# x transposed by DMA on its way into SBUF, in place of TensorE transposes: a gated mix of a state-space layer and a linear-attention layer

## The chip, the cores and the metric

The kernel runs on one core of a Trainium2 chip. The metric is device time in microseconds (us) of one execution. The time before is the median of four runs; one further execution was taken by the hardware profiler, and the views of it that are quoted here all come from that execution.

## The reference, cut to what matters

One input x (2048 rows by 512 columns, bf16) goes through two branches, and a gate per row mixes them.

```python
g = sigmoid((x * gate_w).sum(-1, keepdims=True))
# branch a: diagonal complex state space, 512 states, recurrence over the 2048 rows
Bu = einsum("bld,pd->blp", x, B_bar)
for t in range(L): h = Lam_bar * h + Bu[:, t]
a = 2 * einsum("blp,dp->bld", hs, Cmat).real + x * Dskip
# branch b: linear attention, 32 heads of 16; phi = [softmax(p), softmax(-p)]
q, k, v = split(x @ wqkv);  pq = q @ w_phi;  pk = k @ w_phi     # per head
kv = einsum("bhsf,bhsd->bhfd", phi(pk), v);  z = phi(pk).sum(s)
o = (phi(pq) @ kv) / (phi(pq) . z + 1e-6)
b = o.reshape(B, S, D) @ wo
out = g * a + (1 - g) * b
```

Every matmul that reads x contracts over its 512 columns, so TensorE needs x with the columns on the partitions: that is the tile `xT`.

## The kernel before, in words

**Rows and phases.** Row r is split as r = 4·(128·a + c) + f: f (0 to 3) is the phase, a (0 to 3) the block, c the partition. `xT[:, kt, f*512 + a*128 + c]` holds column block kt of that row, so the columns of `xT` are ordered by phase first. The scan runs over 512 steps of four rows each.

**Loading x.** SP loads x in its natural layout into `xn` (two tiles that share the memory of `ET0` and `ET1`), block 0 in two halves and then blocks 1 to 3 (L312, L315, L317). For each block and phase `x_block` runs four TensorE transposes (L431) into one PSUM buffer, and VectorE or ScalarE copies that buffer into `xT` (L373, L375): 16 groups of four transposes, 16 copies. Ahead of them six matmuls on a zeroed tile (`NWARM`, L418) run while no data is there, and one more (`NDUM`, L443) follows the first two groups.

**What follows on TensorE.** `v_unit` (L457): 16 groups of four 128x512 matmuls, x times Wv; groups 0 and 1 are split in two halves, so that the first can start with half of Wv. `par` (L493 to L498): nine small matmuls that spread the parameter vectors. `gate` (L904): 64 matmuls of one column. `g_unit` (L685, L690): x times `BT`, needs both halves of `BT` and all four blocks of one phase. `fold` (L665): folds w_phi into Wk and Wq; needs `WT` and the block-diagonal `BD` that VectorE makes. Then `k_unit` (L797, L828), `q_unit` (L888), `smalls` (L955) and `mix` (L997, L1013, L1017, L1029) with the output transfers.

**SP's queue at the start.** The x pieces and half of Wv, then six DMA transposes of 512x512 bf16 (512 KB each): the two of B into `BT` (L321), Wk and Wq into `WT` (L323, L324), the two of C into `ET` (L602), with Wc (L322) and four pieces of Wo (L326) among them. DMAs take turns on eight semaphores, so the ninth waits until the first has landed.

**The order.** Nothing is scheduled on the chip. The list `ORDER` gives, task by task, the order of issue and the engine of each task that could go to two; a small planner (`_Plan`) walks it and assigns buffers. Each engine runs its own instructions in that order and waits on semaphores. Constants such as `d_x` are due times of the loads that the planner uses; they are not waits.

Of the kernel before, what the change touches and what calls it, by code (L numbers as in the profile page):

```python
# [122 lines left out]
def kernel(  # L123
# [47 lines left out]
NWARM = 6  # L171
NDUM = 1
ORDER = (
    8, 10, 14, 13, 26, 174, 22, 176, 18, 166, 170, 25, 21, 190, 173, 162, 17, 158, 169, 202, 192, 178, 206, 165,
    0, 194, 222, 204, 197, 226, 28, 224, 160, 209, 30, 230, 32, 198, 233, 250, 96, 210, 218, 234, 34, 201, 228,
    36, 40, 38, 214, 252, 180, 42, 242, 134, 212, 236, 44, 238, 46, 216, 4, 186, 136, 2, 48, 90, 59, 240, 254,
    244, 220, 812, 182, 62, 810, 140, 75, 188, 83, 61, 138, 678, 814, 142, 55, 184, 98, 69, 680, 430, 156, 434,
    144, 432, 816, 258, 146, 66, 56, 64, 436, 262, 438, 81, 342, 265, 818, 256, 334, 70, 260, 337, 346, 148, 348,
    338, 554, 150, 341, 444, 446, 344, 152, 52, 440, 154, 6, 450, 443, 356, 358, 360, 350, 382, 352, 354, 87, 388,
    50, 449, 362, 364, 85, 384, 820, 392, 528, 556, 522, 366, 390, 272, 386, 368, 394, 370, 490, 396, 372, 530,  # L180
    456, 398, 524, 458, 374, 532, 274, 400, 452, 496, 526, 376, 534, 78, 536, 460, 404, 822, 470, 538, 276, 406,
    414, 378, 92, 380, 540, 472, 462, 417, 408, 426, 454, 494, 544, 492, 266, 73, 475, 498, 500, 464, 284, 286,
    546, 410, 542, 502, 476, 298, 466, 412, 77, 504, 548, 620, 428, 100, 506, 508, 102, 288, 104, 88, 562, 268,
    468, 624, 614, 652, 512, 514, 622, 278, 618, 300, 106, 270, 516, 518, 616, 478, 290, 110, 626, 108, 280, 520,
    480, 282, 302, 628, 114, 656, 558, 630, 292, 418, 654, 112, 564, 550, 294, 246, 402, 482, 422, 304, 248, 566,
    560, 646, 116, 568, 738, 650, 648, 574, 484, 632, 118, 552, 486, 570, 576, 636, 424, 572, 580, 658, 594, 586,
    740, 296, 122, 742, 582, 660, 420, 638, 744, 584, 578, 306, 120, 746, 710, 94, 126, 686, 488, 596, 588, 598,
    124, 698, 640, 308, 310, 748, 688, 634, 690, 770, 130, 662, 750, 590, 510, 682, 700, 642, 128, 702, 684, 644,
    776, 664, 712, 774, 778, 838, 692, 668, 592, 752, 312, 772, 754, 314, 780, 782, 600, 714, 832, 694, 756, 670,
    704, 844, 672, 834, 760, 696, 602, 330, 842, 846, 784, 318, 706, 840, 132, 604, 666, 762, 850, 332, 836, 716,  # L190
    708, 718, 786, 720, 826, 322, 606, 788, 852, 722, 874, 854, 792, 848, 868, 320, 326, 794, 862, 674, 608, 724,
    764, 324, 796, 828, 872, 830, 328, 676, 766, 726, 768, 798, 800, 864, 878, 856, 876, 610, 866, 860, 728, 804,
    808, 870, 802, 892, 880, 894, 896, 806, 730, 758, 884, 904, 902, 900, 732, 858, 898, 906, 886, 1268, 908, 316,
    1000, 890, 882, 1270, 998, 910, 1036, 914, 996, 916, 1274, 1002, 734, 1272, 888, 918, 912, 1262, 920, 922,
    1028, 1004, 1054, 924, 1006, 930, 1074, 1062, 1030, 1022, 1008, 1010, 1056, 1128, 1130, 1076, 1080, 1024,
    1048, 1132, 1032, 612, 1264, 1050, 1256, 1126, 1058, 1026, 1266, 1078, 1082, 1100, 1102, 1034, 1012, 1052,
    1114, 932, 736, 1040, 1060, 1106, 1014, 1084, 1104, 1088, 1108, 1016, 1110, 1018, 1112, 1134, 1020, 1260,
    1038, 1086, 942, 936, 1116, 1136, 926, 1138, 934, 1066, 1276, 1064, 954, 1278, 1142, 944, 1092, 1118, 1204,
    1206, 1042, 1210, 1230, 1258, 938, 1232, 1068, 1236, 1208, 1212, 1234, 1044, 1214, 1090, 1152, 928, 1144,
    1146, 1158, 966, 1238, 1094, 1178, 1070, 1120, 1216, 940, 1154, 1218, 1122, 1280, 1148, 1096, 1222, 1240,  # L200
    1073, 1184, 1180, 1242, 1156, 946, 1186, 1284, 1166, 1282, 1160, 1244, 968, 1188, 1286, 1192, 948, 1288, 1246,
    1150, 1290, 1162, 1384, 1292, 1098, 1182, 1168, 1248, 1296, 1364, 1164, 1386, 970, 1190, 1358, 1125, 1170,
    1366, 1194, 1298, 1250, 1390, 956, 1300, 1360, 1220, 950, 958, 1392, 1302, 1224, 1368, 1196, 1312, 1046, 1306,
    1388, 1362, 1394, 1314, 1172, 1370, 1308, 952, 1338, 960, 1396, 1226, 1174, 1198, 1252, 1332, 1310, 1376,
    1200, 1372, 962, 1346, 1398, 1316, 1334, 964, 1400, 1318, 1340, 972, 1304, 1402, 1202, 1416, 1374, 1255, 978,
    1418, 1336, 1320, 1342, 1436, 980, 1438, 1344, 1378, 1404, 1324, 974, 1420, 1229, 1410, 976, 1442, 1380, 1348,
    982, 990, 1412, 1322, 1326, 1444, 1440, 1406, 1462, 1350, 1414, 1177, 984, 1383, 992, 1468, 1494, 1422, 986,
    1446, 1450, 1464, 1448, 988, 1470, 1428, 1352, 1328, 1496, 1354, 1488, 1476, 994, 1330, 1472, 1466, 1490,
    1424, 1454, 1474, 1140, 1498, 1409, 1492, 1500, 1480, 1356, 1426, 1478, 1452, 1430, 1433, 1456, 1482, 1435,
    1502, 1485, 1504, 1506, 790, 1294, 1458, 1514, 824, 1508, 1460, 1520, 1487, 1522, 1516, 1510, 1518, 1513, 1524)  # L210
# [18 lines left out]
def _fast_path(ctx, tc, A_x, A_Lambda_re, A_Lambda_im, A_B_re, A_B_im, A_C_re, A_C_im, A_log_dt, A_Dskip,  # L229
# [5 lines left out]
    x4 = A_x[0].rearrange("(a c f) d -> a c f d", f=F, c=P)  # L235
# [64 lines left out]
    xn2 = [wk.tile([P, 2, F, D], BF16, tag=f"ET{k}", name="xn", bufs=1) for k in range(2)]  # L300
    xn = [xn2[a // 2][:, a % 2] for a in range(4)]
# [10 lines left out]
    nc.sync.dma_start(out=xn[0][:, 0:2], in_=x4[0][:, 0:2])  # L312
    for k, q in ((0, nc.scalar), (2, nc.sync)):
        q.dma_start(out=Wv[:, k:k + 2, :], in_=B_wqkv[k * P:(k + 2) * P, 2 * D:3 * D].rearrange("(k p) n -> p k n", p=P))
    nc.sync.dma_start(out=xn[0][:, 2:4], in_=x4[0][:, 2:4])  # L315
    for a in range(1, 4):
        nc.sync.dma_start(out=xn[a], in_=x4[a])  # L317
# [26 lines left out]
    pl = _Plan({"DVE": 2.4e3, "ACT": 5.0e3, "PE": 1.1e3, "SP": 32.0e3})  # L344
# [10 lines left out]
    early = [pl.held("ET", k) for k in range(4)]  # L355
# [4 lines left out]
    def bfv(b):  # L360
        return b.t[:].bitcast(BF16)[:, 0:512]
# [17 lines left out]
    d_x = [pl.at(t) for t in (3.9, 5.6, 7.0, 8.6, 10.2)]  # L379
    d_wv, d_b, d_wk, d_wq, d_wo, d_ct = (pl.at(t) for t in (5.3, 19.5, 25.5, 30.5, 33.0, 0.0))  # L380
    d_wv0 = pl.at(4.4)
    d_vec, d_wc = pl.at(10.5), pl.at(21.0)
# [38 lines left out]
    xt = {}  # L421
    dums = []

    def x_block(a):
        pl.unit("x_block")
        for f in range(F):
            b = pl.buf(*A1)

            def tr(e, b=b, f=f):
                for kt in range(KT):  # L430
                    nc.tensor.transpose(bfv(b)[:, kt * P:(kt + 1) * P], xn[a][:, f, kt * P:(kt + 1) * P], ident[:])  # L431
            t = pl.add({"PE": 460.0} if a == 0 and f < 2 else _pe(4, 128), tr, deps=[d_x[a + (a > 0 or f > 1)]], follow=[t_warm], bufs=[b, early[a // 2]])
            if a == 0 and f < 2:
                dums.append(t)
            xt[a, f] = evac_task(xT[:, :, tcols(f, a)], b, lambda b: bfv(b).rearrange("p (k c) -> p k c", k=KT), [t],
                                 ("ACT", "DVE"), bf=True, rank=9)

        if a == 0:
            bd = pl.buf(*A1)

            def dum(e):
                for _ in range(NDUM):
                    MM(out=bd.t[:], lhsT=warm[:, 0:P], rhs=warm[:], start=True, stop=True)  # L443
            t_dum.append(pl.add({"PE": NDUM * 430.0}, dum, follow=dums, bufs=[bd]))

    vt = {}
    t_dum = []

    def v_unit(ti):
        pl.unit("v_unit")  # L450
        f, a = ti % F, ti // F
        b = pl.buf(*A1)

        def mm(k0, k1):
            def fn(e):
                for kt in range(k0, k1):
                    MM(out=f32v(b), lhsT=xT[:, kt, tcols(f, a)], rhs=Wv[:, kt, :], start=(kt == 0), stop=(kt == KT - 1))  # L457
            return fn
        if ti < 2:
            t = pl.add({"PE": 860.0 if ti == 0 else 434.0}, mm(0, 2), deps=[xt[a, f], d_wv0], follow=t_dum, bufs=[b])  # L460
            t = pl.add({"PE": 434.0}, mm(2, 4), deps=[d_wv], follow=[t], bufs=[b])
        else:
            t = pl.add(_pe(4, 512), mm(0, 4), deps=[xt[a, f], d_wv], bufs=[b])
        vt[ti] = evac_task(vx[:, ti, :, 0:Dh], b, lambda b: f32v(b).rearrange("p (h e) -> p h e", e=Dh), [t], ("ACT",), rank=8.5)

    x_block(0)
# [366 lines left out]
    x_block(1)  # L833
    for ti in range(0, 4):
        v_unit(ti)
    x_block(2)
# [858 lines left out]
```

## Time and profile before

| | |
|---|---|
| median of 4 runs | 154.82 us (154.78 to 154.97) |
| the profiled execution, its own time | 154.34 us |
| its span in the profile | 152.3 us |
| busy: PE (TensorE matmul) | 145.7 us, 96% of the span |
| busy: DVE (VectorE) | 134.3 us, 88% |
| busy: ACT (ScalarE) | 110.2 us, 72% |
| granted TensorE clock, mean | 0.995 |

Times inside the profile are counted from the start of the span. PE is TensorE's matmuls, PEld its weight loads, which overlap them; SPq is the part of SP that issues DMAs. A group line gives the source line, the engine, the operation, what is written and read, the count, the busy time and the mean length of one in ns. In a table of windows each engine has its busy time and, in brackets, its instructions; the last three columns are the granted clock, the share of the 16 DMA engines that was busy, and the GB/s that they moved. Matmuls are pipelined, so the 379 ns of one 128x512 matmul is its latency; in a stream four of them take 0.86 us.

### The profile page before, as it was taken

To read this page: it belongs to the slowest core of one execution; us is meant where nothing else is said; L and a number is where in the kernel's file an instruction comes from. 1 tells how busy PE (TensorE), PEld (TensorE's weight loads), DVE (VectorE), ACT (ScalarE), POOL (GpSimd) and SP (SyncE) were. 2 spreads that over 40 slices of the span, in tenths; PEclk is the share of its full clock that TensorE was granted. 3 is DMA by queue.
4 is the path that set the end of the run, shared out by engine and by line. 5 is a ranking of instruction groups with operands and counts; after the bars stand their busy time and mean duration, and the time that the engine had idled before them with its cause. 6 is when DMAs were issued, how large, how long until landed. Compare 5 with 4: busy or idle time off the path is not lost.

```text
span 152.3 us, 3284 instructions
## 1 busy us (share of the span) xinstructions
PE 145.7 (96%) x1173; PEld 85.5 (56%) x1173; DVE 134.3 (88%) x377; ACT 110.2 (72%) x226; POOL 4.3 (3%) x14
## 2 busy tenths in 40 slices
PE   6799999999999999999999999999999999999990
PEld 1465476745665656655544665656556555555570
DVE  2377998998999999999999899999999999999250
ACT  3049999889897889879889997977774392753030
POOL 8300000000000000000000000000000000000000
PEclk9999999999999999999999999999999999999998
DMA  4999989300013141334603222244132634316531
GB/s 129 380 274 212 160 229 225 62 0 0 0 31 76 34 93 55 103 82 110 79 0 101 93 94 86 80 87 65 34 104 68 73 75 97 100 37 118 128 103 45
DMA packets 31147, 14.95 MB, mean 98 GB/s; under 512 B 23192, under 2 KB 30488, under 8 KB 31128
## 3 DMA queue, kind: packets, MB, share of 16 engines
q1 hardware_dynamic: 29280, 13.20, 38.2%
q10 hardware_dynamic: 1752, 1.51, 3.4%
q8 instruction: 10, 0.16, 0.5%
q14 instruction: 9, 0.07, 0.2%
q0 software_dynamic: 96, 0.00, 0.0%
HBM read 3.17 MB, written 2.10 MB: 35 GB/s over the span
## 4 chain that ended last, share of the span: by engine, by line
PE 84%; DMA 5%; DVE 5%; ACT 1%; issue 0%; SPq 0%; DVEq 0%
PE pp L685 18%; PE pp L1013 17%; PE pp L1029 9%; PE pp L797 9%; PE pp L457 8%; PE pp L888 5%; PE pp L997 4%; PE pp L690 3%; DMA Wv<-in_B_wqkv_dram 3%; DMA xn<-in_A_x_dram 3%; PE pp L828 3%; PE pp L1017 2%; DVE c L733 2%; PE pp L431 1%; PE pp L665 1%; DVE KVbd L870 1%
## 5 line engine op out<-in xcount | busy, mean ns | idle before, releaser
L685 PE MATMUL pp<-xT,BT 128*128 128x512 bf16 x128 | 31.9, 381 | 0.0
L1000 ACT CAST late<-pp 128x512 bf16<-128x512 f32 x32 | 17.8, 598 | 10.8 <-PE pp L997 10.7
L1013 PE MATMUL pp<-CT,Gs 128*128 128x512 bf16 (+1 forms) x104 | 23.5, 362 | 0.0
L685 PEld LDWEIGHTS <-BT 128*128 128x128 bf16 x128 | 17.8, 145 | 8.7
L242 ACT ACTIVATE E<-pp 128x512 bf16<-128x512 f32 x32 | 17.8, 613 | 2.1 <-PE pp L797 1.5
L242 ACT ACTIVATE ET<-pp 128x512 bf16<-128x512 f32 x32 | 17.7, 603 | 1.0 <-PE pp L888 0.9
L1034 ACT ACTIVATE late<-pp,Gg 128x512 bf16<-128x512 f32 (+1 forms) x15 | 9.5, 669 | 9.8 <-PE pp L1029 9.8
L1029 PE MATMUL pp<-Wo,late 128*128 128x512 bf16 (+1 forms) x68 | 15.9, 367 | 0.0
L457 PE MATMUL pp<-Wv,xT 128*128 128x512 bf16 x64 | 15.8, 379 | 0.1
L888 PE MATMUL pp<-xT,Wq 128*128 128x512 bf16 x64 | 15.8, 378 | 0.0
L797 PE MATMUL pp<-Wk,xT 128*128 128x512 bf16 x64 | 15.4, 379 | 0.0
L373 ACT CAST vx<-pp 128x512 bf16<-128x512 f32 x16 | 9.3, 595 | 7.9 <-PE pp L457 7.8
L1013 PEld LDWEIGHTS <-Gs 128*128 128x128 bf16 x104 | 9.4, 98 | 7.3 <-DVE Gs L773 0.5
L373 ACT CAST Gs<-pp 128x512 bf16<-128x512 f32 x21 | 12.2, 603 | 1.7 <-PE pp L690 1.7
L1004 DVE TENSOR_TENSOR late<-late 128x512 bf16<-128x512 bf16 x32 | 12.3, 417 | 0.0
L997 PE MATMUL pp<-KVbd,ET 128*128 128x128 bf16 x128 | 10.7, 219 | 0.0
L997 PEld LDWEIGHTS <-ET 128*128 128x128 bf16 x128 | 8.6, 98 | 3.4 <-issue 0.2
L797 PEld LDWEIGHTS <-xT 128*128 128x128 bf16 x64 | 6.1, 98 | 6.7
L821 DVE TENSOR_TENSOR E<-E,rc 128x2048 bf16<-128x2048 bf16 x8 | 9.7, 1219 | 0.1
L888 PEld LDWEIGHTS <-Wq 128*128 128x128 bf16 x64 | 5.9, 97 | 6.3
L733 DVE TENSOR_TENSOR_SCAN c<-sp,c 128x512 bf16<-128x512 f32 x8 | 9.3, 1208 | 0.0
L457 PEld LDWEIGHTS <-xT 128*128 128x128 bf16 x64 | 5.8, 98 | 5.8 <-DVE xT L375 0.4
(173 smaller groups left out, 253.5 us busy)
## 6 DMA issues: line engine op xcount, KB each, us to landing
Zs<-c SPq DMA_DIRECT2D x32, 64.0 KB, 2.1
xn<-in_A_x_dram SPq DMA_DIRECT2D x3, 512.0 KB, 4.8
out_dram<-late ACTq DMA_DIRECT2D x9, 128.0 KB, 2.0
c<-c SPq DMA_DIRECT2D x16, 64.0 KB, 2.0
CT<-ET SPq DMA_DIRECT2D x8, 128.0 KB, 3.6
out_dram<-late SPq DMA_DIRECT2D x6, 128.0 KB, 2.0
xn<-in_A_x_dram SPq DMA_DIRECT2D x2, 256.0 KB, 4.4
Wo<-in_B_wo_dram SPq DMA_DIRECT2D x4, 128.0 KB, 2.7
```

Source lines behind the costliest of these rows:

```text
L242: return nc.scalar.activation(**kw)
L373: nc.scalar.copy(out=o, in_=view(b))
L457: MM(out=f32v(b), lhsT=xT[:, kt, tcols(f, a)], rhs=Wv[:, kt, :], start=(kt == 0), stop=(kt == KT - 1))
L685: MM(out=f32v(b), lhsT=BT[:, kt].rearrange("p r (q t) -> p (r q) t", t=NT)[:, :, j + 4 * h], rhs=xT[:, kt, f * NCH:(f + 1) * NCH], start=( ...
L733: nc.vector.tensor_tensor_scan(out=bw_.t[:, ri], data0=rb, data1=b1.t[:, ri], initial=0.0, op0=ALU.mult, op1=ALU.add)
L797: MM(out=f32v(b), lhsT=xT[:, kt, tcols(f, a)], rhs=Wk2[:, kt, :], start=(kt == 0), stop=(kt == KT - 1))
L888: MM(out=f32v(b), lhsT=Wq2[:, kt, g * P:(g + 1) * P], rhs=xT[:, kt, f * NCH:(f + 1) * NCH], start=(kt == 0), stop=(kt == KT - 1))
L997: MM(out=f32v(pn[sgn])[:, g * P:(g + 1) * P], lhsT=ets[f].t[:, sgn, g, cs], rhs=KVbd[:, sgn, g, :], start=True, stop=True)
L1000: tn = pl.add(_act(512), lambda e, sgn=sgn: nc.scalar.copy(out=o2.t[:, sgn], in_=f32v(pn[sgn])), deps=[t], bufs=[pn[sgn], o2], rank=rank + 2)
L1004: VT(out=v, in0=v, in1=als[f].t[:, a, sgn * H:(sgn + 1) * H].rearrange("p (g h) -> p g h", g=HG).unsqueeze(2).to_broadcast([P, HG, Dh, 8]) ...
L1013: MM(out=f32v(py)[:, 0:w], lhsT=st, rhs=CT[:, tt // 2 + 4 * (tt % 2), n * w:n * w + w], start=(tt == 0), stop=False)
L1029: MM(out=f32v(py)[:, 0:w], lhsT=oT.t[:, g, :], rhs=Wo[:, g, hs], start=False, stop=(g == HG - 1))
```

## The change

x no longer comes in its natural layout. SP issues five DMA transposes that write `xT` directly: phase 0 in two halves of 256 rows, then phases 1, 2 and 3 with 512 rows each. A source row is 1 KB, and the rows of one phase lie 4 KB apart. `xn`, the 64 TensorE transposes, the 16 copies of their results and the extra matmul `NDUM` go; `NWARM` rises from 6 to 8. Both halves of Wv are issued by ACT's queue; before, one was issued by SP. Only the first group of `v_unit` is split. `ET0` and `ET1` are free from the start. The list `ORDER` and the planner's due times are new throughout, so that tasks of every engine stand in another order.

```diff
-NWARM = 6
-NDUM = 1
+NWARM = 8
 ORDER = (
...
-    x4 = A_x[0].rearrange("(a c f) d -> a c f d", f=F, c=P)
+    xf = A_x[0].rearrange("(r f) d -> f r d", f=F)
...
-    xn2 = [wk.tile([P, 2, F, D], BF16, tag=f"ET{k}", name="xn", bufs=1) for k in range(2)]
-    xn = [xn2[a // 2][:, a % 2] for a in range(4)]
...
-    nc.sync.dma_start(out=xn[0][:, 0:2], in_=x4[0][:, 0:2])
-    for k, q in ((0, nc.scalar), (2, nc.sync)):
-        q.dma_start(out=Wv[:, k:k + 2, :], in_=B_wqkv[k * P:(k + 2) * P, 2 * D:3 * D].rearrange("(k p) n -> p k n", p=P))
-    nc.sync.dma_start(out=xn[0][:, 2:4], in_=x4[0][:, 2:4])
-    for a in range(1, 4):
-        nc.sync.dma_start(out=xn[a], in_=x4[a])
+    for k in (0, 2):
+        nc.scalar.dma_start(out=Wv[:, k:k + 2, :], in_=B_wqkv[k * P:(k + 2) * P, 2 * D:3 * D].rearrange("(k p) n -> p k n", p=P))
+    for f, r0, r1 in ((0, 0, NCH // 2), (0, NCH // 2, NCH), (1, 0, NCH), (2, 0, NCH), (3, 0, NCH)):
+        nc.sync.dma_start_transpose(out=xT[:, :, f * NCH + r0:f * NCH + r1], in_=xf[f][r0:r1])
...
-    early = [pl.held("ET", k) for k in range(4)]
+    early = {k: pl.held("ET", k) for k in (2, 3)}
...
-    xt = {}
-    dums = []
-
-    def x_block(a):
...
+    xt = {(a, f): d_x[f + (f > 0 or a > 1)] for f in range(F) for a in range(4)}
...
-        if ti < 2:
-            t = pl.add({"PE": 860.0 if ti == 0 else 434.0}, mm(0, 2), deps=[xt[a, f], d_wv0], follow=t_dum, bufs=[b])
+        if ti == 0:
+            t = pl.add({"PE": 860.0}, mm(0, 2), deps=[xt[a, f], d_wv0], follow=[t_warm], bufs=[b])
...
-    x_block(1)
     for ti in range(0, 4):
         v_unit(ti)
-    x_block(2)
     for ti in range(4, 8):
         v_unit(ti)
-    x_block(3)
     for ti in range(8, 12):
         v_unit(ti)
```

In the new order TensorE's stream begins: eight warm matmuls; group 0 of `v_unit` (first half), group 12, group 0 (second half), group 8, all of phase 0; group 9; `par`; groups 13 and 5; group 2; group 1; 16 gate matmuls; groups 7, 3, 11 (phase 3) and 10; 32 gate matmuls; three groups of `g_unit` (12 matmuls, the first that read `BT`); the first `fold` group; 16 gate matmuls; a `fold` group; a `g_unit` group; two `fold` groups. Groups 4, 6, 14 and 15 come later. On SP the fifth piece of x waits, by its semaphore, until the third has landed.

## The prediction, made before the changed kernel was run

> **What bounds the kernel now.** I read the engines' busy shares first, then the windows of the first 32 us, then the start of the chain of waits, then SP's queue. First the busy shares and the slices:
>
> ```profile
> PE 145.7 (96%) x1173; PEld 85.5 (56%) x1173; DVE 134.3 (88%) x377; ACT 110.2 (72%) x226; POOL 4.3 (3%) x14
> PE   6799999999999999999999999999999999999990
> DVE  2377998998999999999999899999999999999250
> ```
>
> TensorE has no idle slice between the third and the last. It sets the end, so a matmul taken out of its stream counts in full, provided that its data keep up. DVE is nearly as full from about 15 us on. The windows (us, PE, PEld, DVE, ACT, POOL, clock, DMA share, GB/s):
>
> ```profile
> 4.00:8.00 4.00, 3.13 (x31) 1.79 (x30) 1.29 (x5) 0.00 (x0) 0.95 (x2) 1.00 1.05 375
> 8.00:12.00 4.00, 3.70 (x45) 2.54 (x44) 2.85 (x13) 2.35 (x5) 0.00 (x0) 1.00 1.13 275
> 12.00:16.00 4.00, 4.00 (x29) 2.11 (x27) 3.66 (x20) 3.93 (x9) 0.00 (x0) 1.00 1.27 173
> 16.00:20.00 4.00, 4.00 (x37) 2.13 (x36) 3.96 (x16) 3.82 (x11) 0.00 (x0) 1.00 1.04 209
> ```
>
> TensorE waits only before 12 us. The DMA engines are already full there: at 375 GB/s while x comes in naturally, at about 200 GB/s while they transpose. The chain says when TensorE stops waiting and what it does then:
>
> ```profile
> 5.39 4.13 DMA xn<-in_A_x_dram
> 9.56 0.84 PE pp L431 x12
> 10.41 0.86 PE pp L457 x4
> 11.27 0.22 PE pp L431 x4
> ...
> 11.87 0.55 PE pp L431 x8
> ```
>
> From 9.56 us on the chain is TensorE almost without a break. The group of the transposes, SP's issues, and two times from issue to landing:
>
> ```profile
> L431 PE MATMUL pp<-ident,xn 128*128 128x128 bf16 x64 | 5.3, 222 | 1.1 <-DMA xn<-in_A_x_dram 1.1
> 10.68 1.70 SPq L321 DMA_TRANSPOSE BT<-in_A_B_im_dram  x1
> 16.32 2.39 SPq L324 DMA_TRANSPOSE WT<-in_B_wqkv_dram  x1
> 21.48 2.05 SPq L602 DMA_TRANSPOSE ET<-in_A_C_re_dram  x1
> BT<-in_A_B_im_dram SPq DMA_TRANSPOSE x1, 5.9
> ET<-in_A_C_re_dram SPq DMA_TRANSPOSE x1, 4.7
> ```
>
> Six 512 KB transposes are in the kernel already. They price the new ones: SP spends 2.05 to 2.39 us on issuing one that does not wait.
>
> **TensorE's useful stream.** The last matmul of the last tile ends at 148.10 us (L1029 starts at 147.06 and takes 1.04). From 9.56 that is 138.54 us. Of it 32 transposes are 2.05 us (0.84+0.22+0.55+0.22+0.22 in the chain). Eight Wv matmuls were done before 9.56, worth 8 x 0.216 = 1.73. Useful work is 138.54 - 2.05 + 1.73 = 138.2 us. Before, it has an effective start of 148.1 - 138.2 = 9.9 us; the change is worth what it takes off that.
>
> **The new start.** The warm matmuls begin at 1.27 and come 0.43 us apart, so eight end at about 4.7. The first Wv group needs the first half of Wv (landed by about 4.6 before) and 256 rows of x. Transposed, these land no earlier than the natural 256 KB did (3.9: the first transpose starts then) and hardly later than the second Wv half (5.39 in the chain), with which they share the engines. I take 4.9. Two matmuls later (5.3) the stream needs the second half of phase 0; the first 1 MB, Wv and phase 0, should be in between 5.4 and 6.1, and I take 5.8: a wait of 0.5.
>
> **The queue behind it.** Until the first matmul on BT five more 512 KB pieces have to land: phases 1, 2, 3 and both parts of B. Call the time of one c. Bounds: 2.05, the shortest issue that did not wait, and 2.65. The latter is the whole stretch from 9.56 to 28.1 (where traffic ends in windows of half a us), 18.5 us less 2.6 for issuing Wo, over six pieces. The landings in the trace's semaphore records sit around the lower end: B_re 2.1 us after the last of x, Wq 1.9 after Wk, C_im 2.2 after C_re; B_im took 3.6, during which a 16 KB instruction fetch, one packet in the trace, took 1.2 us. I take c = 2.2, since most rows lie there, and allow one such fetch (1.4) as an even chance. The 4 KB pitch of x's rows is not in the trace; Wk and Wq, whose rows lie 3 KB apart, are the nearest and show no surcharge. The fifth piece waits for the third's landing (about 8 us), two pieces ahead of its turn: no cost. So B_im lands at 5.8 + 5 x 2.2 = 16.8, with a fetch 18.2, at c = 2.65 at 19.1, at c = 2.05 at 16.1.
>
> TensorE's work before BT is 12 Wv groups (48 x 0.216 = 10.37), par (0.16) and 48 gate matmuls (3 x 0.38 = 1.14): 11.7 us. It is ready at 4.9 + 0.5 + 11.7 = 17.1. Hence BT matmuls start at 17.1, or with a fetch at 18.3; the useful work left is 138.2 - 11.7 = 126.5. The end of matmuls is 143.6 or 144.8, that is 4.5 or 3.3 us earlier than 148.1. At c = 2.65 it is 19.2 + 126.5 = 145.7, a gain of 2.4. Wk follows B_im by Wc and one piece, 2.4 in all; the three BT groups (2.6) hide that. BD comes out of DVE in time if DVE's parameter chain starts early too: it was done at 22.3, 10.4 us after par's results; now par is at about 9 us, and the mask and swap steps (0.9 us) stand ahead of it, so about 19, with fold due at 19.7.
>
> **The other engines.** The 11 copies on DVE (421 ns each) and 5 on ACT (584 ns) mostly filled idle time: only two on DVE and three on ACT come after par's results. DVE: par's results move from 11.9 to about 9.4, 2.5 us; two copies (0.8), the setup steps moved ahead of par (1.2) and 0.7 of PSUM copies that the new list gives to ACT go, 1.0 of small scalings comes: it can end 2.5 + 0.8 + 1.2 + 0.7 - 1.0 = 4.2 us earlier. ACT: the first Wv copy moves from 8.85 to about 7; three copies go (1.75), two of the folds come (1.2): about 2.4 us earlier in the stretch up to 40 us, where it was busy for 28.9 of 31.2 us. So ACT and DVE allow 2.4 to 4.2 and nearly bind. I charge 0.4 us for waits in the new order that the trace of before cannot show; the bounds are 0 and 2. Ten output transfers went through ACT's queue and seven through SP's; SP now issues five more, 0.53 us each, among transposes of 1.2 us, where it is not full: nothing. C's load lands near 28 as before and is first used at 44.9: nothing. The tail behind the last matmul keeps its form: nothing.
>
> **One rule against, one beside.** Four TensorE transposes take 0.22 us in the stream, 55 ns each, while c is 2.2 us for 16 blocks of 128x128, 138 ns each, on engines that do nothing else at that time. The Trainium skill, "VectorE: DVE Perf Modes", § Rules for kernel authors, says to use TensorE for a 128x128 transpose where a PSUM destination will do; § The three transpose paths gives 390 ns for it and 1309 ns for the DMA. By those figures, taken one at a time, x's 64 blocks would cost the DMA 84 us (an estimate) and the kernel would be far slower; the rows of B, W and C contradict that.
>
> The Trainium skill, "DMA: Bandwidth & Descriptors", § Latency and other measured facts, gives 261 GB/s for a DMA transpose whose middle dimension is not contiguous: 2.0 us a piece, an estimate, by which TensorE would never wait for BT and the gain would be the full 4.5.
>
> **The sum.** Midway between 4.5 and 3.3 is 3.9, less 0.4: 3.5 us. The profiled execution would go from 154.34 to 150.8. The median of the runs was 0.48 above that execution, so I forecast 154.82 - 3.5 = 151.3.
>
> **Rivals.** (1) *Another engine takes over.* DVE is busy for 3.9 to 4.0 of every 4 us between 44 and 60, ACT for 28.9 of 31.2 before 40; TensorE then meets full PSUM buffers or late exps, and only 0.3 to 2.5 us remain: 152.3 to 154.5. For it: the two sums above. Against: both engines also lose work. (2) *The transposed queue is too slow: slower than before.* If the 4 KB pitch, Wv's share or further fetches bring c over 3.1, BT matmuls start after 5.8 + 5 x 3.1 = 21.3, and 126.5 more passes 148. At B_im's own 3.6 they start at 23.8, the matmuls end at 150.3, and the time is 157.0. For it: that one piece. Against: the other five. (3) *No change*, where c is just 3.1 or DVE does not move. That the change does not do what it says can be left out: the new TensorE stream has 63 fewer matmuls, 64 transposes and one extra less two warm ones.
>
> **How the numbers follow.** Forecast (gain 2.5 to 4.8): 0.52. Rival 1: 0.30. No change: 0.04. Rival 2: 0.14. About 0.2%, or 0.3 us, is what a measurement can tell from no change. The range runs from 150.0 (all gains, no waits) to 154.2, which takes in most of rival 1; the forecast's own range is 150.0 to 152.3. Faster 0.82, same 0.04, slower 0.14.
>
> **What would show it.** Right: no L431, first Wv matmul near 4.9, BT matmuls at 17 to 18.3, TensorE full from there, last matmul near 144.6. Wrong: the phases of x landing over 2.7 us apart, TensorE waiting on xT or BT for more than 2 us, or new waits of TensorE on ACT or DVE after 20 us.

## The result: 0.2% slower, and where TensorE waits now

The changed kernel takes 155.13 us (median of 34 runs, 154.15 to 156.34), the kernel before 154.81 on the same chips; the ratio is 1.0022 [1.0011, 1.0034]. The forecast was 151.3, its range ended at 154.2. The profiled execution took 154.94, its span is 152.9.

Two lines of the page of the changed kernel, busy time and TensorE's slices:

```profile
PE 142.8 (93%) x1110; PEld 82.1 (54%) x1110; DVE 128.9 (84%) x368; ACT 108.5 (71%) x219; POOL 4.5 (3%) x14
PE   6489999999999999999999699989999999999990
```

The 64 transposes are gone and TensorE is busy for 2.9 us less, but its row now has lower slices: 4 and 8 at 4 to 12 us, where they were 7 and 9, and a 6 near 87 us, where it was 9. The windows name the stretches (columns as before: us, PE, PEld, DVE, ACT, POOL, clock, DMA share, GB/s):

```profile
4.00:8.00 4.00, 1.59 (x6) 0.23 (x4) 0.76 (x9) 0.00 (x0) 1.21 (x2) 1.00 1.21 251
8.00:12.00 4.00, 3.61 (x24) 1.67 (x23) 0.00 (x0) 0.89 (x2) 0.00 (x0) 1.00 0.99 224
84.00:92.00 8.00, 6.75 (x62) 3.35 (x59) 7.79 (x18) 6.16 (x13) 0.00 (x0) 1.00 0.30 98
```

The last stretch in the kernel before:

```profile
84.00:92.00 8.00, 8.00 (x124) 5.03 (x121) 7.41 (x19) 7.10 (x15) 0.00 (x0) 1.00 0.29 95
```

In 4 to 8 us TensorE works for 1.59 us where it worked for 3.13, and in 84 to 92 for 6.75 where it worked for 8.00. TensorE's timeline tells what each idle time waited for (start, length, line, what, count, and in brackets the idle time ahead and its releaser):

```profile
1.27 3.59 PE L411 MATMUL pp<-warm 128*128 128x512 bf16 x8 [1.27 <-DVE warm L305]
6.41 0.60 PE L426 MATMUL pp<-Wv,xT 128*128 128x512 bf16 x2 [1.54 <-DMA xT<-in_A_x_dram]
7.88 3.20 PE L426 MATMUL pp<-Wv,xT 128*128 128x512 bf16 x14 [0.86 <-DMA xT<-in_A_x_dram]
11.46 0.17 PE L461 MATMUL pp<-ident,vec_n 20*128 20x20 bf16 x1 [0.39 <-issue]
...
20.03 2.79 PE L653 MATMUL pp<-xT,BT 128*128 128x512 bf16 x12
23.16 0.40 PE L633 MATMUL pp<-BD,WT 128*128 128x128 bf16 x4 [0.34 <-DMA WT<-in_B_wqkv_dram]
...
87.89 0.95 PE L920 MATMUL pp<-SM,ET 128*128 128x16 bf16 x32 [1.25 <-ACT ET L240]
...
103.20 1.04 PE L994 MATMUL pp<-Wo,late 128*128 128x512 bf16 x4 [0.39 <-DMA late<-late]
```

The first matmul on x starts at 6.41 (forecast 4.9), the first on BT at 20.03 (17.1 to 18.3), and four later waits add 0.39 + 0.34 + 1.25 + 0.39. The last Wo matmul ends at 148.73 (144.6). ScalarE's queue shows the 0.39 ahead of par in the making:

```profile
6.39 0.25 ACTq L313 DMA_DIRECT2D vec_n<-in_A_Lambda_im_dram  x1
7.85 0.26 ACTq L313 DMA_DIRECT2D vec_n<-in_A_Dskip_dram  x1
8.15 0.49 ACTq L313 DMA_DIRECT2D vec_n<-in_gate_w_dram  x1
```

In the semaphore records the first and second piece of x land at 6.37 and 7.83, 0.02 us before: two of the five 1 KB parameter loads wait for the large pieces whose semaphores they take next, and the fifth stands behind them on the queue. Its own semaphore was free from 4.30 on; it lands at 11.26, and par starts at 11.46. And VectorE's timeline shows what comes ahead of the smalls group (L920), which needs SM:

```profile
83.55 0.69 DVE L691 TENSOR_TENSOR c<-c,Tcs 128x1024 bf16<-128x1024 bf16 x1 [1.22 <-DMA c<-c]
...
85.67 0.43 DVE L835 TENSOR_TENSOR KVbd<-pp,mask 64x256 bf16<-64x256 f32 x1
...
87.58 0.16 DVE L838 TENSOR_TENSOR SM<-pp,mask 64x16 bf16<-64x16 f32 x1
```

The kv matmuls end at 84.05, but VectorE first waits for a transfer of its scan and runs four steps of it; SM is done at 87.74, and TensorE goes on at 87.89. The releaser that the timeline names, ScalarE's ET, ended 0.13 us after SM; the waits of e4 below name SM, and in e15, where SM is early, the smalls start at 85.66 without a wait, while the same run of exponentials goes on to 87.06.

### The profile page after: what moved, and what is told of

Same layout as the page of the kernel before. It is cut to its first block, busy times and chain, and to the rows that moved or that the text cites. A ratio compares the mean times of both kernels' runs of the same rounds, so it can differ in the third digit from the quotient of the medians.

```text
span 152.9 us, 3142 instructions
## 1 busy us (share of the span) xinstructions
PE 142.8 (93%) x1110; PEld 82.1 (54%) x1110; DVE 128.9 (84%) x368; ACT 108.5 (71%) x219; POOL 4.5 (3%) x14
## 4 chain that ended last, share of the span: by engine, by line
PE 78%; DMA 10%; SPq 7%; ACT 1%; issue 0%; DVE 0%
PE pp L978 16%; PE pp L653 16%; PE pp L994 9%; PE pp L765 9%; PE pp L853 8%; PE pp L962 5%; DMA WT<-in_B_wqkv_dram 4%; DMA xT<-in_A_x_dram 4%; PE pp L658 3%; SPq L311 3%; SPq L315 3%; PE pp L796 3%; DMA late<-late 3%; PE pp L426 2%; PE pp L920 2%; PE pp L982 2%
## 5 line engine op out<-in xcount | busy, mean ns | idle before, releaser
L653 PE MATMUL pp<-xT,BT 128*128 128x512 bf16 x128 | 31.3, 380 | 0.0
L240 ACT ACTIVATE E<-pp 128x512 bf16<-128x512 f32 x32 | 17.0, 614 | 1.4 <-PE pp L796 1.3
L426 PE MATMUL pp<-Wv,xT 128*128 128x512 bf16 x64 | 15.1, 379 | 2.4 <-DMA xT<-in_A_x_dram 2.4
L999 ACT ACTIVATE late<-pp,Gg 128x512 bf16<-128x512 f32 (+1 forms) x15 | 10.1, 679 | 8.4 <-PE pp L994 8.2
L765 PE MATMUL pp<-Wk,xT 128*128 128x512 bf16 x64 | 15.9, 379 | 0.0
L969 DVE TENSOR_TENSOR late<-late 128x512 bf16<-128x512 bf16 x32 | 12.8, 416 | 0.3 <-ACT late L965 0.3
L367 ACT CAST Gs<-pp 128x512 bf16<-128x512 f32 x19 | 10.9, 591 | 1.7 <-PE pp L658 1.0
L962 PE MATMUL pp<-KVbd,ET 128*128 128x128 bf16 x128 | 11.2, 219 | 0.0
```

What stands on the lines that cost most here:

```text
L240: return nc.scalar.activation(**kw)
L367: nc.scalar.copy(out=o, in_=view(b))
L653: MM(out=f32v(b), lhsT=BT[:, kt].rearrange("p r (q t) -> p (r q) t", t=NT)[:, :, j + 4 * h], rhs=xT[:, kt, f * NCH:(f + 1) * NCH], start=( ...
L765: MM(out=f32v(b), lhsT=xT[:, kt, tcols(f, a)], rhs=Wk2[:, kt, :], start=(kt == 0), stop=(kt == KT - 1))
L962: MM(out=f32v(pn[sgn])[:, g * P:(g + 1) * P], lhsT=ets[f].t[:, sgn, g, cs], rhs=KVbd[:, sgn, g, :], start=True, stop=True)
L969: VT(out=v, in0=v, in1=als[f].t[:, a, sgn * H:(sgn + 1) * H].rearrange("p (g h) -> p g h", g=HG).unsqueeze(2).to_broadcast([P, HG, Dh, 8]) ...
```

## The experiments

Theory: the removal is worth what was forecast, and it was spent on a later start and on waits of the new order. Rivals: the removal was never worth it, because VectorE or ScalarE would have set the end; or the transposing queue as such is too slow. "Before" is each time the kernel before on the same chip in the same runs. Where an experiment lists no other base, its edit is to the changed kernel.

### The removal alone

**e3.** The kernel before, without the transposes and their copies; Wv reads the natural x, and xT holds a constant from GpSimd.

```diff
-                    nc.tensor.transpose(bfv(b)[:, kt * P:(kt + 1) * P], xn[a][:, f, kt * P:(kt + 1) * P], ident[:])
+                pass
+    nc.gpsimd.memset(xT[:], 0.01)
```

> The kernel before with its own order and its natural load of x, but without the 64 TensorE transposes and the 16 copies: the early Wv groups read the natural tile as if it were transposed, and all later readers of xT get a constant, so the values are wrong. It prices the removal alone. If TensorE's stream is all that counts, what was spent on transposes after 9.56 us (2.05 us) and part of what stood before it goes: 151 to 152.7. If ScalarE or VectorE bind, less than 1 us: above 153.8.

155.81 (1.0054 [1.0036, 1.0072]). It tells nothing of the removal: the large memset held up VectorE's setup, par waited 3.30 us for `sel`, and the clock fell to half for the matmuls that followed. e7 is the same with xT filled from the other two engines.

**e7.**

```diff
+    nc.vector.memset(xT[:, 0:2], 0.01)
+    for kt in (2, 3):
+        for h in range(4):
+            nc.scalar.activation(out=xT[:, kt, h * 512:h * 512 + 512], in_=warm[:], func=ACT.Exp)
```

> The kernel before with its own order list and natural loads of x, but without the 64 TensorE transposes and the 16 copies: xT is filled with a constant instead (half by VectorE, half by ScalarE, before x lands), so its values are not x's. This is the removal alone, with no transposing DMA for x and no new order. Theory 'the matmuls removed count in full on TensorE's stream, and the loss came with the additions': TensorE saves 64 x 55 ns = 3.5 us less what its data make it wait, and the median is 151.0 to 152.8. Rival 'VectorE or another engine would have taken over anyway, so the removal was never worth 3.5 us': 153.5 to 154.6, with new waits of TensorE after 20 us.

153.09 (152.23 to 154.30), 0.986 [0.9806, 0.9915]. The six runs are two groups: 152.23 to 152.25 at a mean granted clock of 0.996 or more, and 153.94 to 154.30 at 0.986. The profiled execution is of the second group; its wait of TensorE on ScalarE, and two of its windows:

```profile
PE pp L459 <- ACT vx L377: 1.6, 1, 1.6
```

```profile
8.00:12.00 4.00, 2.37 (x16) 1.30 (x15) 2.15 (x18) 3.21 (x10) 0.00 (x0) 0.90 1.07 254
84.00:92.00 8.00, 7.89 (x110) 4.80 (x110) 7.41 (x19) 7.01 (x17) 0.00 (x0) 1.00 0.28 89
```

At full clock the removal is worth 155.06 - 152.24 = 2.8 us (three executions), although the fill put 1.6 us of waiting on ScalarE into the start. After 26 us TensorE waits for nothing in the old order: VectorE and ScalarE let this much through. The first rival falls, up to 2.8 us.

### The start

**e1.** x by plain DMA of the same sizes (xT then holds rows, not columns).

```diff
-        nc.sync.dma_start_transpose(out=xT[...], in_=xf[f][r0:r1])
+        nc.sync.dma_start(out=xT[...], in_=A_x[0][f * NCH + r0:f * NCH + r1, :]...)
```

> The changed kernel with its own order, but x comes by plain DMA: the same five pieces of the same size, not transposed, so the values are wrong. Three theories of where the forecast gain went. Q (queue): x lands late because it is transposed, and every later wait follows from that. Then the first Wv matmul starts near 4.9 us instead of 6.41, the first fold near 20 instead of 23.16, the waits at 86 to 88 and 103 us are gone, the last matmul ends near 144.5 instead of 148.7, and the time is near 150.9. P (parameters): the small parameter loads come late and hold back VectorE and ScalarE; then par still starts after 9.5 us, the late waits of 1.7 us stay, and the time is near 152.5. O (order): the new list has its late waits whatever lands when; they stay or grow, 152.5 to 154.

157.83, 1.0201 [1.0155, 1.0246]. The first two pieces land at 4.90 and 6.58 instead of 6.37 and 7.83, so transposing costs 1.2 to 1.5 us there. But the kernel is slower, since ScalarE's queue waits as before, and longer (two lines of the queue, then TensorE's):

```profile
4.92 0.25 ACTq L314 DMA_DIRECT2D vec_n<-in_A_Lambda_im_dram  x1
6.61 0.25 ACTq L314 DMA_DIRECT2D vec_n<-in_A_Dskip_dram  x1
```

```profile
14.10 0.17 PE L462 MATMUL pp<-ident,vec_n 20*128 20x20 bf16 x1 [2.65 <-issue]
```

par waits 2.65 us for parameter loads that were issued at the landings of x, the last at 8.91. So e1 does not price the transposing in the kernel's time: what it brings forward is lost at par. The late wait is there too (1.3 us), so it does not come from the transposes of x.

**e2.** No parameter loads by DMA: `vec_n` is filled with a constant.

```diff
-    for n, src in enumerate(vsrc):
-        nc.scalar.dma_start(out=vec_n[4 * n:4 * n + 4, :], in_=src.rearrange("(j p) -> j p", p=P))
+    nc.vector.memset(vec_n[:], -0.5)
```

> The changed kernel without the five small loads into vec_n: a memset gives constants instead, so the parameters are wrong. With them go their five semaphore turns, so no piece of x waits for another to land. Q: par starts right behind the Wv groups, near 10.9 us instead of 11.46, the last piece of x lands near 13.5 instead of 14.35, a gain of 0.5 to 0.8 us: 154.3 to 154.6. P: VectorE's and ScalarE's chains start earlier, the late waits of 1.7 us go too: 152.8. O: as Q.

154.83, 0.9992 [0.9969, 1.0015], against 1.0022 for the changed kernel: the turns cost 0.3 us by the medians, hardly more than the intervals. The wait at par is gone, but par comes hardly earlier (11.33) in the profile, since most of the 16 matmuls ahead of it ran at half clock:

```profile
6.18 5.22 PE L425 MATMUL pp<-Wv,xT 128*128 128x512 bf16 x16 [1.31 <-DMA xT<-in_A_x_dram]
```

Until 9.4 us they start 0.42 us apart, then 0.21. The late wait stays at 1.3.

**e4.** Wv is not loaded but filled with a constant.

```diff
-    for k in (0, 2):
-        nc.scalar.dma_start(out=Wv[:, k:k + 2, :], in_=...)
+    nc.vector.memset(Wv[:], 0.01)
```

> The changed kernel with Wv filled by a memset instead of its two loads (wrong values). If sharing the DMA engines with Wv is what delays phase 0 (landings 6.39 and 7.85 us), they land near 4.9 and 6.2, the first Wv matmul starts near 5 and the time falls by 1.5 to 2 us, to 153.3. If a transposed piece is slow to start by itself, the first lands after 5.7 and the time falls by less than 0.8 us.

153.01, 0.9868 [0.9826, 0.9909]. The first two pieces of x land at 4.34 and 5.50, where the prediction had put them (4.9 and 5.8); TensorE's timeline, then its waits:

```profile
4.66 3.37 PE L425 MATMUL pp<-Wv,xT 128*128 128x512 bf16 x12
...
21.18 0.40 PE L632 MATMUL pp<-BD,WT 128*128 128x128 bf16 x4
```

```profile
PE pp L919 <- DVE SM L837: 1.2, 1, 1.2
PE pp L993 <- DMA late<-late: 0.6, 1, 0.6
```

Everything up to fold is 1.7 to 2.0 us earlier, the late waits are as before (1.2 and 0.6), and the time is 2.1 us less. Wv's two loads are the largest single cost. That the landings moved is their traffic and not the semaphore turns, since the first two pieces wait for no turn in either kernel; but without the two loads the parameter loads go out by 3.05 us as well, and the wait at par is gone, so the 2.1 us hold both. x is still transposed here, so the second rival, a queue too slow as such, falls for the start.

**e6.** Wv's second half on SP behind the first piece of x; the five parameter loads on GpSimd.

```diff
+        if r1 < NCH:
+            wvd(nc.sync, 2)
...
-        nc.scalar.dma_start(out=vec_n[4 * n:4 * n + 4, :], ...)
+        nc.gpsimd.dma_start(out=vec_n[4 * n:4 * n + 4, :], ...)
```

> The changed kernel with the loads at the start re-queued: the second half of Wv is issued by SP right behind the first piece of x, and the five parameter loads and three gate vectors go to GpSimd's queue, so that they no longer take a turn on the semaphores that the x pieces also use. Theory 'the start was lost to the plain Wv traffic beside the first transposes and to the semaphore turns': the first piece lands by 5.0 instead of 6.39, the first Wv matmul starts by 5.2, par runs at about 10 instead of 11.46, the matmuls on BT start 1 us earlier, and the median is 153.5 (152.8 to 154.2). Rival 'a transposed piece needs its 2.3 us of start-up and 2 us of work whatever else is queued': the second half of x lands later by what Wv is moved behind, about 8.5, TensorE waits there instead, and the median is 154.8 to 155.8.

157.35, 1.0113 [1.007, 1.0156]: the rival. The first piece lands at 5.27, the second only at 8.62:

```profile
8.66 5.96 PE L429 MATMUL pp<-Wv,xT 128*128 128x512 bf16 x14 [2.74 <-DMA xT<-in_A_x_dram]
```

The first Wv matmul starts at 5.32, but the wait moved to the second half of phase 0 and grew, and 14 matmuls then take 5.96 us instead of 3.20, because the clock was at half from 7.46 to 14.29 us.

**e14.** e4, and the two transposes of B left out (BT holds a constant).

```diff
-        nc.sync.dma_start_transpose(out=BT[:, :, ri, :], in_=B_)
+    nc.vector.memset(BT[:].rearrange("p k r q -> p (k r q)"), 0.01)
```

> e4_no_wv_traffic (Wv filled with a constant instead of loaded), and in addition the two transposes of B are left out and BT is filled with a constant by VectorE. TensorE's work is the same; the transposing queue has two 512 KB pieces less ahead of Wk. Theory 'the transposing queue sets fold's start': Wk lands near 16 to 17, TensorE runs from 4.7 to fold without waiting for data, fold starts at 19.7 to 20.3 (e4: 21.18) and the median is 151.6 to 152.1 with the late wait still in it. Rival 'TensorE or VectorE's BD set fold's start, the queue is only close': fold stays at 20.8 to 21.3, median 152.7 to 153.1.

154.09, 0.9973 [0.994, 1.0005], so 1 us slower than e4. It does not decide its question: the fill kept VectorE from `sel`, for which par waited 0.68 us; par ended at 11.2 and fold came at 21.97, with no wait for data from par on. Whether the queue would bind a TensorE that is ready earlier it cannot say.

### The late stage

**e5.** Two q_unit groups go ahead of smalls, two scan steps behind KVbd/SM.

```diff
 ORDER:
-    ... 786, 658, 698 ... 772, 660, 732 ... 736, 792 ... 826, 834 ... 666, 800, 802, 804, 806
+    ... 786, 698 ... 772, 732 ... 736, 658, 660, 792 ... 826, 800, 806, 834 ... 666, 802, 804
```

> The changed kernel with four entries of the order list moved, and nothing else: two q_unit groups of TensorE go ahead of the smalls group that waited 1.25 us near 87 us, and two steps of VectorE's scan chain, which themselves waited 1.22 us for a transfer, go behind the KVbd/SM step that the smalls group needs. Theory 'the new order has waits of its own' (1.25 + 0.4 us of the lost gain): the wait of the smalls group falls from 1.25 to under 0.3 us, the last Wo matmul ends near 147.5 and the median is 153.8 (153.4 to 154.2). Rival 'VectorE or ScalarE sets the end whatever the order of these four': the same 1.2 us come back as waits on VectorE within the next 20 us, and the median stays at 154.8 to 155.3.

155.81, 1.0036 [1.0011, 1.0062]. The wait near 87 is gone, and 1.04 us came back at 94, on ScalarE's exponentials (0.81 and then 0.23):

```profile
94.09 0.26 PE L920 MATMUL pp<-SM,ET 128*128 128x16 bf16 x4 [0.81 <-ACT ET L240]
```

**e13 and e15.** Two kernels with 14 warm matmuls (e8 below); e15 moves the two scan steps as e5 does, and leaves TensorE's order alone.

> e8_warm14 once more, as the base of e15 and e16 on the same chip. If its gain is the clock's, 153.8 (0.99 of before) again. If e8 was a lucky draw of the transposing queue, whose landings differ by up to 1 us from run to run, 154.2 to 154.8.

> e13 with two entries of the order list moved: the first two steps of VectorE's scan chain (which wait 1.22 us for a transfer) go behind the KVbd/SM step; TensorE's order stays. Theory 'the late wait of the smalls group is VectorE's order': SM is done at 86.3 instead of 87.74, smalls start at once behind the q_unit groups near 86.7, the 1.25 us wait is gone, the scan that follows starts 0.4 us later, and the median falls by 0.8 to 1.2 us against e13. Rival 'ScalarE's twelve exponentials, which end at the same moment, hold it': the wait stays at 1.0 or more and the median is e13's within 0.3 us.

e13 took 153.86 (0.9932 [0.9907, 0.9958]), e15 154.33 (0.9979 [0.9957, 1.0002]): not faster. In e15 SM is done at 85.4 and smalls do not wait, but the next link does; lines of VectorE, ScalarE and TensorE in e15:

```profile
87.42 2.33 DVE L703 TENSOR_TENSOR_SCAN c<-sp,c 128x512 bf16<-128x512 f32 x2
...
91.00 0.42 DVE L933 TENSOR_TENSOR q<-pp,q 128x256 f32<-128x256 f32 x1
```

```profile
91.78 0.40 ACT L242 ACTIVATE q<-q,eps_t 128x128 f32<-128x128 f32 x1 [2.53 <-DVE q L936]
```

```profile
92.72 0.26 PE L922 MATMUL pp<-SM,ET 128*128 128x16 bf16 x4 [0.96 <-ACT ET L242]
```

The small step q (L933), ready at 87.8, stands behind VectorE's scan until 91.00; ScalarE waits 2.53 us for it with the next exponentials queued behind; TensorE waits 1.19 us for those (0.96 and then 0.23). In the new order the scan of 4 us lies between the q_unit stage and what feeds it. Whichever side the two steps are put on, about 1.2 us is lost.

### Warming

**e8.** 14 warm matmuls instead of 8; e13 is the same kernel.

```diff
-NWARM = 8
+NWARM = 14
```

> The changed kernel with 14 warm matmuls instead of 8, so that TensorE is busy until about 6.2 us instead of 4.87. Theory 'in part of the executions the idle 1.5 us ahead of the first Wv matmul costs the granted clock, and up to eight matmuls run 0.43 us apart instead of 0.22': the clock stays full from 4.3 us on, the spread of the runs narrows, and the median falls by 0.3 to 0.8 to 154.3 to 154.9. Rival 'the clock comes back at once and the gap costs nothing': median 155.0 to 155.4.

153.83 and 153.86; 0.9914 [0.9882, 0.9945] and 0.9932 [0.9907, 0.9958]. Both are under either kernel, so this one line makes the change worth having. The first real matmul starts at 6.28 in e13 and the third at 7.59:

```profile
7.59 3.19 PE L426 MATMUL pp<-Wv,xT 128*128 128x512 bf16 x14 [0.70 <-DMA xT<-in_A_x_dram]
```

From fold to 103 us the matmuls of e13 stand 0.20 us ahead of the changed kernel's, one by one, and 0.75 us after it, since the wait of 0.39 is not there: a 16 KB instruction fetch that fell among the transposes of `late` in the changed kernel (at 101.12) comes ahead of them here (98.49). That is 0.75 us of the 1.3 by which the medians differ.

**e9.** The kernel before with `NWARM` 10 instead of 6.

> The kernel before with 10 warm matmuls instead of 6, nothing else. It asks whether the gain of e8_warm14 (1.3 us against the changed kernel) belongs to the change's idle gap or to any kernel here. Theory 'the gap ahead of the first Wv matmul is the change's own': before has no such gap (its transposes start at 3.90, the warm matmuls end at 4.0), so the median stays within 0.3 us of 154.8 to 155.1, or rises by up to 0.5 because the first transposes start later. Rival 'more warming helps every kernel': at least 0.6 us less.

154.78, 1.0006 [0.9986, 1.0026]: the kernel before has nothing to gain there.

**e17 and e18.** The first has 14 warm matmuls of 292 columns (the time of eight, the code of 14), the second six as they were and four in float32 (the time of about 14, meant to have the instruction count of eight).

```diff
-            MM(out=bw.t[:], lhsT=warm[:, 0:P], rhs=warm[:], start=True, stop=True)
+            MM(out=bw.t[:, 0:292], lhsT=warm[:, 0:P], rhs=warm[:, 0:292], start=True, stop=True)
```

```diff
+            if n >= 6:
+                MM(out=bw.t[:, 0:256], lhsT=warm[:].bitcast(F32)[:, 0:P], rhs=warm[:].bitcast(F32), start=True, stop=True)
```

> The changed kernel with 14 warm matmuls of 292 columns instead of 8 of 512: the same columns in all, so TensorE is idle from 4.9 to the first piece of x as before, but the program has the 12 more instructions of e13. Theory 'the place of the instruction fetch': the fetch near 101 us moves ahead of the transposes of late, the wait of 0.39 us at 103 is gone, and the median is 153.9 to 154.5. Rival 'the time of warming': as the changed kernel, 154.8 to 155.4, with runs at a lower mean clock.

> The changed kernel with six warm matmuls as they were and four in float32 with 256 columns, which need no weight loads of their own: as many TensorE instructions as in the changed kernel, but TensorE stays busy until about 6 us (if a float32 column takes four times as long). Theory 'the place of the instruction fetch': the fetch stays near 101 us, the wait at 103 stays at 0.3 to 0.6, and the median is 154.7 to 155.2. Rival 'the time of warming': 153.7 to 154.2.

154.87 (1.0014 [0.9991, 1.0037]) and 154.54 (0.9995 [0.9966, 1.0024]). In e17 the fetch came at 99.56 and the wait at 103 was gone, and still the time is the changed kernel's: the place of the fetch alone is not the gain. Its profiled execution shows what the gap can cost, in its matmuls and in a window with the granted clock at 0.50:

```profile
7.61 4.88 PE L426 MATMUL pp<-Wv,xT 128*128 128x512 bf16 x14 [0.81 <-DMA xT<-in_A_x_dram]
```

```profile
8.00:11.00 3.00, 3.00 (x8) 1.03 (x7) 0.00 (x0) 0.00 (x0) 0.00 (x0) 0.50 0.96 209
```

In e18 the fetch moved too (98.46), so it does not part the two: the trace lists eight weight loads and eight matmuls for its four float32 ones, and as many TensorE records in all as for e17. Its 154.54 is 0.6 us under the changed kernel, not the full 1.3.

The profiled executions speak for the time of warming. Of the five that have x as changed and 3.3 to 3.6 us of warm matmuls (changed kernel, e2, e5, e6, e17), four ran many of the first Wv matmuls at half clock: e2 until 9.4 us, e5 from 8.44 to 11.85, e6 from 7.46 to 14.29, e17 from 7.92 to 11.34. Of the seven with 14 warm matmuls (e8, e10 to e13, e15, e16) none did. Of 36 executions of the changed kernel 26 had a mean clock of 0.993 or more, and their median is 155.05; but this cannot rule the clock out, since e2's execution is listed at 1.000: half clock before the clock's first rise is not counted. What the clock does not explain are e18 and the four kernels that follow.

**e10, e11, e12, e16.** With 14 warm matmuls: the parameter loads on GpSimd's queue (e10), Wv's second half on SP ahead of x (e11), both (e12), and e11 with the scan steps of e15 (e16).

```diff
-        nc.scalar.dma_start(out=vec_n[4 * n:4 * n + 4, :], ...)
+        nc.gpsimd.dma_start(out=vec_n[4 * n:4 * n + 4, :], ...)
```

```diff
-    for k in (0, 2):
-        nc.scalar.dma_start(out=Wv[:, k:k + 2, :], in_=...)
+    for k, q in ((0, nc.scalar), (2, nc.sync)):
+        q.dma_start(out=Wv[:, k:k + 2, :], in_=...)
```

> e8_warm14 with the five parameter loads moved from ScalarE's queue to GpSimd's, right behind the identities, so that they take no turn on the semaphores that the x pieces use. Theory 'the turns cost: three of these loads waited for landings of x and Wv (par at 11.07 with 0.46 us of waiting ahead of it), and the fifth piece of x waited for the third's landing': the fifth piece is issued about 0.7 us earlier, Wk lands at 22.4 instead of 23.1, the waits ahead of par (0.46) and fold (0.72) shrink to under 0.3 together, and the median falls from 153.83 to 153.1 (152.9 to 153.4). Rival 'what is gained at par and fold is lost at the late wait, whose time is set by ScalarE's exponentials and VectorE': median 153.6 to 153.9.

> e8_warm14 with the second half of Wv issued by SP ahead of the first piece of x (ScalarE's queue keeps the first half), so that both halves load during the 2.3 us in which the first transpose moves nothing. Theory 'plain packets of Wv beside the transposes hold the first piece's landing': Wv's second half lands by 4.8, the first piece of x by about 5.7 and the second by 7.0; the first Wv matmul starts at 6.2 (the warm matmuls' end) instead of 7.00, later pieces come 0 to 0.5 us later than in e8_warm14, and the median is 153.2 to 153.8. Rival 'SP's 0.6 us of issuing ahead of the transposes delays every piece by as much': fold waits 0.6 us longer and the median is 154.0 to 154.6.

> The edits of e10_warm14_params_pool and e11_warm14_wv_ahead together: the candidate for a version that beats both kernels. If both costs are real and add up, 152.7 (152.4 to 153.3), with the first Wv matmul at 6.2, par by 10.2 and no wait of TensorE over 0.3 us before 26 us; what remains is the late wait of 1.2 us near 87. If the late stage absorbs them, 153.5 to 153.9.

> e15 with the second half of Wv issued by SP ahead of the first piece of x (as in e11). If the start and the late wait are both bounds of their own, 152.7 to 153.2; if the transposing queue sets fold's start whatever TensorE does before, it equals e15 within 0.4 us.

154.57, 154.63, 154.75 and 154.75 (0.9972 to 0.9995): none keeps e8's gain. e11 shows why an earlier start does not carry: the first matmul is at 5.83, 0.6 us earlier than in the changed kernel, but the second piece holds the next until 7.58, and those on BT wait for B, which lands at 20.01 (changed kernel 19.87):

```profile
7.58 3.20 PE L426 MATMUL pp<-Wv,xT 128*128 128x512 bf16 x14 [1.14 <-DMA xT<-in_A_x_dram]
...
20.14 2.78 PE L653 MATMUL pp<-xT,BT 128*128 128x512 bf16 x12 [0.80 <-DMA BT<-in_A_B_im_dram]
```

## Why the prediction was wrong, point by point

**The useful stream was right.** From the first BT matmul 126.5 us of work were forecast. 20.03 to 148.73 is 128.70; less the waits (0.34 + 1.25 + 0.39) it is 126.7. And e7 (2.8 us) bears out that the removal counts.

**The step that failed first is the new start.** "Hardly later than the second Wv half, with which they share the engines. I take 4.9", and 5.8 for the rest of phase 0. Measured: landings at 6.37 and 7.83. Beside Wv's loads the first piece's packets ran from 3.01 to 4.73, in e4 from 2.16 to 3.50; and its semaphore came 1.64 us after the last of them (0.84 in e4), only when Wv's second half (packets from 4.46 to 5.41) had landed at 6.11. Without Wv's traffic the landings are 4.34 and 5.50 (e4). Sharing was counted as bandwidth, and it cost 2.0 us; why the semaphore came so late is not shown.

**par was mis-sized.** "Now par is at about 9 us": 11.46. From the second piece to BT 11.3 us were forecast and 12.15 measured, of which 0.39 is the wait and some 0.3 par's own nine matmuls (0.45 for 0.16). The semaphore turns were weighed for the fifth piece of x ("no cost"; it was issued 0.3 us late), and not for the parameter loads, which take turns on the same semaphores. VectorE's parameter chain therefore starts at 12.02, not 2.5 us earlier. Together the two terms put BT at 20.03, 2.3 us behind the middle of the forecast's 17.1 and 18.3.

**The queue's pace was about right.** From the second piece on, the next four landed 1.91, 2.01, 2.58 and 2.03 us apart (2.58 is the fifth piece, which waited for the third's landing). B's second part took 3.51 and Wk, with Wc ahead, 3.24, each with an instruction fetch in it (8 KB at 18.25 for 0.63 us, 16 KB at 20.70 for 0.98 us). From the second piece to B it is 12.0 us, and 12.4 were forecast with a fetch. "The three BT groups hide" Wk fell short by 0.34. The lower bound, 2.05 as "the shortest issue that did not wait", was misread: the 1.70 us of B's second issue, quoted above it, did not wait either (its semaphore was free from 7.29 on), and three of the measured steps lie under 2.05. Beyond the 0.34 at fold the queue did not hold TensorE up, but it stood close behind: B's second part landed at 19.87, 0.16 us before the first matmul on it, and where TensorE was ready earlier it waited 0.72 (e8) and 0.86 us (e12) for Wk and 0.80 (e11) for B.

The Trainium skill, "DMA: Bandwidth & Descriptors", § Latency and other measured facts, gives 261 GB/s, 2.0 us a piece (an estimate); this agrees with the undisturbed pieces and not with the last two.

**The charge for new waits was too small.** 0.4 was taken, bounds 0 and 2; measured are 1.25 + 0.39 = 1.64, so inside the bounds, 1.2 over. It is rival 1 in small: VectorE's sequence, not its load. That waits of this size are the new order's shows in every kernel that has it, x transposed or not (1.0 to 1.3 us near 87 or 94), and in none with the old one (before, e3, e7 and e9).

**The sum.** 2.3 (start and par) + 0.3 (fold) + 1.2 (late) = 3.8 of the 4.1 us between 144.6 and 148.73. Rival 2, the queue too slow, gave the right sign for a reason that did not hold: c stayed at 1.9 to 2.6 outside the pieces with a fetch, and B was not the bound. (Its turning point was a little off, too: at c = 3.1 its own sum is 147.8, not past 148.)

**What stays open.** How much of the 1.3 us of 14 warm matmuls is the clock: the profiled changed kernel had it full from 5.46 us on, and against that execution e8 and e13 are only 0.6 to 0.75 ahead. And why the gain goes when the loads are re-queued as well; that Wk and B then hold TensorE (0.80 and 0.86 us in e11 and e12) is part of it at most, since e8 waits 0.72 too. Whether the transposed loads with an order like the old one would avoid the late wait was not tried: the old order takes x block by block, and the transposes bring it phase by phase.

## What to carry to other kernels

Transposing by DMA in place of a full TensorE saves TensorE's time, but the first landing sets the start: plain traffic beside the first transposed pieces delays them (e4), though moving it to another place in the queues did not pay here (e6, e11); and price a landing by a row with the same neighbours, not by bandwidth. A small load that takes its turn on a shared set of semaphores waits for whatever large one had the turn before; look for late issues on the queue's own timeline. With an order list that is new throughout, expect the waits it puts in, and when one is moved away, follow the chain to the next link before counting it. Where the first data come late, let the warm matmuls run on until they are there (here 1.3 us by the medians, unless the loads were re-queued too), and look at the spacing of the first matmuls: an execution's mean clock can hide a slow start.

## What the runs showed that was not expected

- A gap of 1.4 to 1.5 us between the warm matmuls and the first real ones was free in one execution (14 matmuls in 3.20 us, changed kernel) and cost 1.7 us in others (4.88 us, e5 and e17), where the clock was at half for 3.41 and 3.42 us. The Trainium skill, "TensorE: Matmul & The Clock Gate", § Part 1, tells of an activity window of 3.4 us that runs freely; the two stretches have that length, and that a shorter gap costs now and then fits it. Its advice to avoid gaps above about 3.4 us does not cover it.
- The first packet of the first transposing DMA moved 2.3 us after its issue began (issued 0.73, first packet 3.01), and 1.4 us where Wv was not loaded (e4, e14: 0.74 or 0.73, then 2.16): the silence at the start is not a fixed price.
- An instruction fetch of 16 KB (about 1 us) can fall into a transpose. In the changed kernel one at 101.12 lay in the transposes of `late` that TensorE waited for until 103.20; with 12 more instructions at the start (e13) it came at 98.49, and the wait was gone.
- A fill of a large tile by GpSimd (e3) or VectorE (e14) in the first 10 us made par wait 3.30 and 0.68 us for `sel`: a constant that stands for a load needs an engine, too.
